# An FFT filter followed by a gated feed-forward network: another order of the loads, the filter loaded step by step, the last transform stage of the first batch two iterations later

## The chip, the cores and the metric

The kernel runs on one core of one Trainium2 chip. The metric is the device time of one execution in microseconds (us); the median of several executions is compared. A core has five engines that run side by side, each with its own queue of instructions in a fixed order: TensorE (PE in the profile; PEld are its weight loads), VectorE (DVE), ScalarE (ACT), GpSimd (POOL) and SyncE (SP), which here only issues loads and the stores of the result. Matmuls write to PSUM, and ACT or DVE bring the results from there to SBUF. Data come from and go to HBM by DMA.

## What is computed

The input `x` has 8 batches of 3136 rows of 256 numbers. Each batch is transformed along its rows, multiplied by a complex filter, transformed back, and goes through a feed-forward network with a convolution over three rows and a gate:

```python
X = np.fft.rfft(x, axis=1)
F = (filt_r + 1j * filt_i)[None, :, :]
y = np.fft.irfft(X * F, n=x.shape[1], axis=1)
...
h = np.maximum(y @ w_in, 0.0)
conv_out = np.zeros_like(h)
for k in range(K):
    conv_out += conv_w[k][None, None, :] * hp[:, k:k + S, :]
gate = 1.0 / (1.0 + np.exp(-conv_out))
return (h * gate @ w_out).astype(np.float32)
```

Here `hp` is `h` with a row of zeros at each end. The weights `w_in`, `conv_w` and `w_out` arrive as 64-bit floats; the kernel turns them into 32-bit floats itself.

## The kernel before

The kernel has two parts. The forward part does the transforms and the filter for all eight batches; the feed-forward part then goes through the result in 28 blocks. This study is about the forward part and the seam between the two.

**The pipeline of the forward part.** A transform of 3136 points is done in stages, as matmuls with tables. The work is cut into pairs of columns: `NP = 14` pairs for each of 8 batches make 112 steps, and one loop with the counter `i` runs all stages at once, each on another step. With `m = i - SKEW` and `SKEW = 15`, iteration `i` does:

- `filt` of step `m - 2`: three products on DVE (L350 to L352) of the transformed rows with the filter tiles `t1_sb` and `t2_sb`, then a sum `z` on POOL (L354);
- `third` of step `m - 4` on PE (L361), with the table `i1_sb`; its result goes to `store`, an ACT copy (L305) and a DMA to `b_dram` issued by ACT;
- `first` of step `i - 1` on PE (L315), of a pair of x rows with the table `s1_sb`; `keep` brings it to the tile `turn` by ACT (L319);
- `second` of step `m - 1` on PE (L338, and L341 for a batch's last step);
- `turn` of step `m` on PE (L326), a transposition with `eye_sb`; `turned_rows` brings it to the tile `a` by ACT (L331).

A batch is transposed only when all 14 of its steps have gone through `first`, which is why `m` lags by 15. The compute engines' order is written out by hand (`manual_schedule`): it is the order of the calls in an iteration. On PE that is `third`, `first`, `second`, `turn`; on ACT `store`, `keep`, `turned_rows`, and then whatever the iteration adds. SP's loads follow the order of the program too. A load waits until its buffer is free and until an earlier load has released its semaphore.

**The loads.** A pair of x rows is `[112, 2, 256]`, and there are `XBUFS = 7` buffers. Seven pairs are loaded ahead of the loop; iteration `i` then loads pair `i + 6`, into the buffer that `first` of pair `i - 1` sets free. The table `s1_sb` comes in seven parts of four columns: four of them ahead of the loop, the others in iterations 1 to 3 (L389). Four small constants come in iteration 4 (L393 to L396). The filter comes in seven chunks of four columns, in every second iteration from 8 on: `fr` into `t1_sb[0:64]`, `fi` into `t2_sb[0:64]` (L252), and the same columns of `i1_sb` (L400). `copy_filter` makes a second copy of each part in partitions 64 to 119 by ACT (L256, and L257 with the sign changed). It is called in every second iteration from 12 on, after `turned_rows`:

```python
def copy_filter(c):
    sl = slice(4 * c, 4 * c + 4)
    nc.scalar.activation(t1_sb[64:120, sl], t1_sb[0:56, sl], AF.Copy)
    nc.scalar.activation(t2_sb[64:120, sl], t2_sb[0:56, sl], AF.Copy, scale=-1.0)
    if c == 6:
        nc.sync.dma_start(out=t1_sb[92:93, G - 1], in_=nyq)
```

Step `p` of each batch uses columns `2p` and `2p + 1` of the filter, in iteration `p + 17` for the first batch; the columns then stay for the other batches.

**The weights.** `convert_conv` and `convert_weights` are generators: each call of `next` does one small step of a conversion on DVE, ACT or POOL and returns, so that one step falls into each iteration. The convolution weights are loaded and converted in iterations 3 to 15; the other weights come in 8 blocks of two 256 KB loads, the first two of them in iteration 16, and are converted from iteration 22 on, eleven calls for a block. Two buffers `raw` serve all these loads.

**The seam.** The feed-forward part reads the finished rows `y`. For the seven later batches the last transform stage runs within the feed-forward part. For batch 0 it runs at the end of the forward loop: from iteration `done = NP * B + 2 = 114` on, `last_load` reads a piece back from `b_dram`, `last_stage` (L216 on PE) transforms it one iteration later, and `last_out` brings it to `y` one more iteration later, the upper part by ACT (L147) and the rest by DVE (L150). There are 14 pieces. The forward steps end in iteration 130 with the last `third`. The first matmuls of the feed-forward part (L178 to L180) read all of `y` of batch 0. At iteration `done` the buffers of the forward part's loads and of the conversions are given up, and `y` takes their room.

Of the kernel before, what the change touches and what calls it, by code (L numbers as in the profile page):

```python
# [13 lines left out]
AF = mybir.ActivationFunctionType  # L14
ALU = mybir.AluOpType

S = 3136
N1 = 112
N2 = 28
G = 28  # L20
D = 256
# [103 lines left out]
def tile_fft_filter_gated_ffn(  # L125
# [2 lines left out]
    x: bass.AP,  # L128
    fr: bass.AP,
    fi: bass.AP,  # L130
    nyq: bass.AP,
    w_in: bass.AP,
    conv_w: bass.AP,
    w_out: bass.AP,
# [8 lines left out]
    nc = tc.nc  # L143
# [85 lines left out]
    with (  # L229
# [13 lines left out]
            nc.gpsimd.memset(v[32:64], 0.0)  # L243
        t1_sb = fc.tile([120, G, D], F32, name="t1_sb")
        t2_sb = fc.tile([120, G, D], F32, name="t2_sb")

        rows = {}

        def load_filter(c):
            sl = slice(4 * c, 4 * c + 4)  # L250
            for t, src in ((t1_sb, fr), (t2_sb, fi)):
                nc.sync.dma_start(out=t[0:64, sl], in_=src[:, sl])  # L252

        def copy_filter(c):
            sl = slice(4 * c, 4 * c + 4)
            nc.scalar.activation(t1_sb[64:120, sl], t1_sb[0:56, sl], AF.Copy)  # L256
            nc.scalar.activation(t2_sb[64:120, sl], t2_sb[0:56, sl], AF.Copy, scale=-1.0)  # L257
            if c == 6:
                nc.sync.dma_start(out=t1_sb[92:93, G - 1], in_=nyq)

        raws = {}

# [5 lines left out]
        def convert_conv():  # L268
            n = 3 * NF
            raw = cv.tile([128, 2, 512], I32, name="raw")  # L270
            nc.sync.dma_start(out=raw[:, 0, 0:2 * n], in_=conv_w)
            yield
            em = cv.tile([128, 2, 512], I32, name="em", bufs=1)
            yield from to_f32(cw.rearrange("p k f -> p (k f)"), raw[:, 0, 0:2 * n], em[:, 0, 0:n], em[:, 1, 0:n])

        def convert_weights():

            for k in range(8):
                raw = raws.pop(k)
                em = cv.tile([128, 2, 512], I32, name="em", bufs=1)  # L280
                ws = cv.tile([128, 2, 256], F32, name="ws")
                yield from to_f32(ws.rearrange("p t n -> p (t n)"), raw.rearrange("p t n -> p (t n)"), em[:, 0], em[:, 1])
                yield
                parts = [[t.rearrange("p a b -> p (a b)")[:, 256 * k:256 * k + 256] for t in w] for w in (wi, wo)]
                for part, (wh, wl) in enumerate(parts):
                    hi_act(wh, ws[:, part])
                yield
                for part, (wh, wl) in enumerate(parts):
                    lo_pool(wl, ws[:, part], wh)
                    yield  # L290
                if k < 6:
                    load_weights(k + 2)

# [4 lines left out]
        def load(b, p):  # L298
            r = xp.tile([112, 2, D], F32, name="x", bufs=XBUFS)
            nc.sync.dma_start(out=r, in_=x[b].rearrange("(p n) d -> p n d", n=N2)[:, 2 * p:2 * p + 2])  # L300
            rows["x", b, p] = r
# [62 lines left out]
        def at(i):  # L364
            return divmod(i, NP) if 0 <= i < NP * B else None

        XBUFS = 7
        SKEW = NP + 1
        nc.sync.dma_start(out=s1_sb[:, 0:4], in_=s1[:, 0:4])
        load(0, 0)  # L370
        load(0, 1)
        for c in range(1, 4):
            nc.sync.dma_start(out=s1_sb[:, 4 * c:4 * c + 4], in_=s1[:, 4 * c:4 * c + 4])
            for p in range(2 * c, min(2 * c + 2, XBUFS)):
                load(0, p)
        csteps, wsteps = convert_conv(), convert_weights()
        done = NP * B + 2
        NI = done + N2 // 2 + 3
        with tc.manual_schedule(engines=COMPUTE):
            for i in range(NI):  # L380
                m = i - SKEW
                if i == done:
# [2 lines left out]
                    forward_pools.close()  # L385
                    yps.append(ctx.enter_context(tc.tile_pool(name="y_even", bufs=1, side="right", reuse_waits="tile")))
                    lp = ctx.enter_context(tc.tile_pool(name="lp", bufs=2, side="right", reuse_waits="tile"))
                if 1 <= i < 4:
                    nc.sync.dma_start(out=s1_sb[:, 4 * i + 12:4 * i + 16], in_=s1[:, 4 * i + 12:4 * i + 16])  # L389
                if (bp := at(i + XBUFS - 1)) and i:  # L390
                    load(*bp)
                if i == 4:
                    nc.sync.dma_start(out=eye_sb, in_=eye)  # L393
                    nc.sync.dma_start(out=s2_sb, in_=s2[:, 0:120])
                    nc.sync.dma_start(out=s2s_sb, in_=s2s[:, 0:120])
                    nc.sync.dma_start(out=m2_sb, in_=m2)  # L396
                if 8 <= i < 22 and i % 2 == 0:
                    sl = slice((i - 8) // 2 * 4, (i - 8) // 2 * 4 + 4)
                    load_filter(i // 2 - 4)
                    nc.sync.dma_start(out=i1_sb[:, sl], in_=i1[:, sl])  # L400
                if bp := at(m - 2):
                    filt(*bp)
                pt = third(*bp) if (bp := at(m - 4)) else None
# [7 lines left out]
                    keep(*at(i - 1), pf)  # L411
                if pa is not None:
                    turned_rows(*at(m), pa)
                if 3 <= i < 16:
                    next(csteps, None)
                if i == 16:
                    load_weights(0)
                    load_weights(1)
                if i >= 22:
                    next(wsteps, None)  # L420
                if 12 <= i < 26 and i % 2 == 0:
                    copy_filter(i // 2 - 6)
                c = 2 * (i - done)
                if 0 <= c - 4 < N2:
                    last_out(0, c - 4)
# [155 lines left out]
```

## Time and profile before

| | us |
|---|---|
| median of 3 runs | 1576.35 |
| lowest and highest of them | 1575.82, 1579.54 |
| the profiled execution | 1574.98 |
| its span, first to last instruction | 1573.2 |

The profile describes the profiled execution; times in it count from the start of its span. The chain of work that ended last is 94% PE and 2% DMA. The loads that matter below, with their sizes and the median time from issue to landing, are these (a KB is 1024 bytes):

| load | count | KB each | us to landing |
|---|---|---|---|
| pair of x rows | 112 | 224 | 2.9 |
| `fr`, a chunk | 7 | 256 | 8.0 |
| `fi`, a chunk | 7 | 256 | 8.2 |
| `i1`, a chunk | 7 | 210 | 7.0 |
| `s1`, a part | 7 | 196 | 6.5 |
| weights, each load | 16 | 256 | 3.5 and 3.8 |
| store to `b_dram` | 112 | 224 | 2.5 |

In a view of the waits, a row names the waiting engine, the tile and line, what it waited for, and then the total in us, the number of waits and the longest. In a view of the timeline a row has its start, its duration, the engine, the line, the operation with its tiles and shapes, and in brackets how long the engine was idle before it and what ended that. Consecutive instructions of one kind stand in one row, with their count. A matmul row's duration reaches into the next row's, because matmuls are pipelined.

### The profile page before, as it was taken

How to read it: one execution, taken by the hardware profiler on the slowest of the kernel's cores; microseconds unless marked ns; L12 is line 12 of the kernel's file. 1: busy time of each engine (PE TensorE's matmuls, PEld its weight loads, DVE VectorE, ACT ScalarE, POOL GpSimd, SP SyncE). 2: the span in 40 equal slices, each digit the busy share in tenths (PEclk: the TensorE clock that was granted, in tenths of full speed). 3: DMA queues.
4: the chain of work that ended last, by engine and by line, in shares of the span. 5: the costliest groups of instructions: out<-in, count | busy, mean ns of one | idle time of the engine just before them, and what ended most of it. 6: DMA issues, size and time to landing. Idle time of an engine off the chain costs nothing.

```text
span 1573.2 us, 27760 instructions
## 1 busy us (share of the span) xinstructions
PE 1545.7 (98%) x10320; PEld 1425.4 (91%) x10320; DVE 1280.8 (81%) x1965; ACT 1249.4 (79%) x2274; POOL 697.9 (44%) x624
## 2 busy tenths in 40 slices
PE   6999999999999999999999999999999999999998
PEld 6777887777999999999999999999999999999998
DVE  0677788778888888888888888888888888888887
ACT  4655555556988888888888888888888888888887
POOL 0455555543444444444444444444444444444444
PEclk8999999999999999999999999999999999999999
DMA  9855555544111011111101111111111111100001
GB/s 226 231 177 164 165 166 165 153 124 129 30 47 48 30 48 48 47 48 47 44 29 36 48 48 52 43 48 48 36 42 48 48 40 38 48 24 24 24 24 48
DMA packets 87209, 115.58 MB, mean 73 GB/s; under 512 B 7114, under 2 KB 59043, under 8 KB 87075
## 3 DMA queue, kind: packets, MB, share of 16 engines
q1 hardware_dynamic: 72739, 88.11, 18.8%
q10 hardware_dynamic: 14336, 25.70, 5.8%
q8 instruction: 82, 1.34, 0.4%
q14 instruction: 52, 0.43, 0.1%
HBM read 62.40 MB, written 51.38 MB: 72 GB/s over the span
## 4 chain that ended last, share of the span: by engine, by line
PE 94%; DMA 2%; ACT 1%; DVE 1%; SPq 0%; issue 0%; POOL 0%; ACTq 0%; POOLq 0%
PE ps_h L179 12%; PE ps_h L180 12%; PE ps_h L178 11%; PE po L488 11%; PE po L490 11%; PE po L489 11%; PE ps L361 6%; PE pp L338 6%; PE ps_h L216 6%; PE ps L315 5%; PE ps L326 3%; DMA t_sb<-in_fi 1%; PE ps L216 1%; DVE y L150 1%; ACT y L147 0%; DMA x<-in_x 0%
## 5 line engine op out<-in xcount | busy, mean ns | idle before, releaser
L153 POOL TENSOR_TENSOR g<-t,g 128x448 fp32r<-128x448 f32 x448 | 517.3, 1155 | 664.5 <-ACT g L147 261.4
L488 PE MATMUL po<-wo,g 128*128 128x256 f32 x1568 | 442.1, 282 | 0.0
L490 PE MATMUL po<-wo,g 128*128 128x256 f32 x1568 | 434.4, 277 | 0.0
L489 PE MATMUL po<-wo,g 128*128 128x256 f32 x1568 | 434.2, 277 | 0.0
L462 DVE SCALAR_TENSOR_TENSOR t<-ps_h,cw,t 128x448 f32<-128x448 f32 x448 | 305.7, 682 | 82.7 <-ACT t L457 72.1
L179 PE MATMUL ps_h<-y,wi 128*128 128x450 f32 x896 | 330.2, 369 | 3.9 <-DVE y L150 3.9
L178 PE MATMUL ps_h<-y,wi 128*128 128x450 f32 x896 | 329.0, 367 | 2.0 <-DVE t L468 1.8
L180 PE MATMUL ps_h<-y,wi 128*128 128x450 f32 x896 | 328.6, 367 | 0.0
L463 DVE SCALAR_TENSOR_TENSOR t<-ps_h,cw,t 128x448 f32<-128x448 f32 x448 | 306.5, 684 | 16.0
L457 ACT ACTIVATE t<-ps_h,cw 128x448 f32<-128x448 f32 x448 | 284.8, 636 | 42.1 <-ACT ps_h L455 1.1
L488 PEld LDWEIGHTS po<-wo,g 128*128 128x128 f32 x1568 | 294.9, 188 | 6.9
L489 PEld LDWEIGHTS po<-wo,g 128*128 128x128 f32 x1568 | 294.6, 188 | 5.6
L490 PEld LDWEIGHTS po<-wo,g 128*128 128x128 f32 x1568 | 294.7, 188 | 0.0
L468 DVE TENSOR_TENSOR t<-ps_h,t 128x448 f32<-128x448 f32 x448 | 275.3, 614 | 0.1
L455 ACT ACTIVATE ps_h<-ps_h 128x450 f32<-128x450 f32 x448 | 251.6, 562 | 29.3 <-PE ps_h L180 24.6
L467 ACT ACTIVATE t<-t 128x448 f32<-128x448 f32 x448 | 255.0, 569 | 12.2 <-DVE t L463 11.0
L147 ACT ACTIVATE g<-t 128x448 fp32r<-128x448 f32 x448 | 254.6, 568 | 0.2 <-DVE t L468 0.2
L354 POOL TENSOR_TENSOR z<-u,v 120x512 f32<-120x512 f32 x112 | 157.2, 1404 | 186.4 <-DVE v L352 171.9
L180 PEld LDWEIGHTS ps_h<-y,wi 128*128 128x128 f32 x896 | 168.2, 188 | 13.7
L179 PEld LDWEIGHTS ps_h<-y,wi 128*128 128x128 f32 x896 | 168.2, 188 | 12.5 <-DVE y L150 5.9
L178 PEld LDWEIGHTS ps_h<-y,wi 128*128 128x128 f32 x896 | 170.2, 190 | 10.2 <-DVE t L468 2.9
L150 DVE TENSOR_TENSOR y<-ps_h,y 128x448 fp32r<-128x448 f32 x98 | 103.3, 1054 | 77.1 <-ACT y L147 77.1
(54 smaller groups left out, 1661.5 us busy)
## 6 DMA issues: line engine op xcount, KB each, us to landing
x<-in_x SPq DMA_DIRECT2D x112, 224.0 KB, 2.9
b_dram<-sb ACTq DMA_DIRECT2D x112, 224.0 KB, 2.5
br<-b_dram SPq DMA_DIRECT2D x112, 224.0 KB, 2.6
out<-ot SPq DMA_DIRECT2D x27, 896.0 KB, 4.1
raw<-in_w_in SPq DMA_DIRECT2D x8, 256.0 KB, 3.5
raw<-in_w_out SPq DMA_DIRECT2D x8, 256.0 KB, 3.8
t_sb<-in_fr SPq DMA_DIRECT2D x7, 256.0 KB, 8.0
t_sb<-in_fi SPq DMA_DIRECT2D x7, 256.0 KB, 8.2
```

What stands on the lines that cost most here:

```text
L153: nc.gpsimd.tensor_tensor(out=dst, in0=src, in1=hi.bitcast(F32), op=ALU.subtract)
L178: nc.tensor.matmul(ps, lhsT=wh, rhs=rh, start=start, stop=False, **kw)
L179: nc.tensor.matmul(ps, lhsT=wh, rhs=rl, start=False, stop=False, **kw)
L180: nc.tensor.matmul(ps, lhsT=wl, rhs=rh, start=False, stop=stop, **kw)
L457: nc.scalar.activation(t, h[:, 1:SUB + 1], AF.Copy, scale=cw[:, 1, f:f + 1])
L462: nc.vector.scalar_tensor_tensor(out=t, in0=h[:, 0:SUB], scalar=cw[:, 0, f:f + 1], in1=t, op0=ALU.mult, op1=ALU.add)
L463: nc.vector.scalar_tensor_tensor(out=t, in0=h[:, 2:SUB + 2], scalar=cw[:, 2, f:f + 1], in1=t, op0=ALU.mult, op1=ALU.add)
L467: nc.scalar.activation(t, t, AF.Sigmoid)
L468: nc.vector.tensor_mul(t, h[:, 1:SUB + 1], t)
L488: nc.tensor.matmul(o, lhsT=gh[:, sl], rhs=wo[0][:, f], start=first, stop=False, skip_group_check=True)
L489: nc.tensor.matmul(o, lhsT=gh[:, sl], rhs=wo[1][:, f], start=False, stop=False, skip_group_check=True)
L490: nc.tensor.matmul(o, lhsT=gl[:, sl], rhs=wo[0][:, f], start=False, stop=last, skip_group_check=True)
```

## The change

The order of the loads, their sizes and some places in the loop change. No stage computes anything else, except at one point named below.

- **First loads.** `s1` and the x rows are issued in turn by one function, two pairs of x rows after each part of `s1`, from the first to the last part.
- **Constants.** `eye` and `s2` are loaded in iteration 8 instead of 4, `s2s` and `m2` in iteration 16.
- **Filter.** It is loaded by steps of two columns instead of chunks of four, one step in each iteration from 10 to 23. `fi` goes into partitions 0 to 55 of `t2_sb`, as before but without the eight rows of padding. `fr` goes into partitions 64 to 119 of `t1_sb`; only for the last step is it loaded into both halves, as the two differ there (so the separate load of `nyq` goes). The copy of `fi` to the other half stays on ACT; the copy of `fr`, now from the upper to the lower half, moves to DVE. Both are made in iteration `p + 16`, one before the step is used. The rows 32 to 63 of `t1_sb` are set to zero by POOL at the start.
- **Weights.** The convolution weights are loaded in iteration 26, with two iterations of pause, and get eight calls. Five of these now do a conversion step; the last three of the eight steps (two on DVE, one on POOL), which add the lowest bits, are not reached. The other weights are loaded from iteration 30 and converted from iteration 35, ten calls for a block instead of eleven: the two subtractions on POOL fall into one iteration.
- **Last stage of batch 0.** `done` is 116 instead of 114. The loop has two iterations more.

```diff
+        nc.gpsimd.memset(t1_sb[32:64], 0.0)
...
-        def load_filter(c):
-            sl = slice(4 * c, 4 * c + 4)
-            for t, src in ((t1_sb, fr), (t2_sb, fi)):
-                nc.sync.dma_start(out=t[0:64, sl], in_=src[:, sl])
+        def load_filter(p):
+
+            sl = slice(2 * p, 2 * p + 2)
+            nc.sync.dma_start(out=t2_sb[0:56, sl], in_=fi[0:56, sl])
+            nc.sync.dma_start(out=t1_sb[64:120, sl], in_=fr[64:120, sl])
+            if p == NP - 1:
+                nc.sync.dma_start(out=t1_sb[0:56, sl], in_=fr[0:56, sl])
+            nc.sync.dma_start(out=i1_sb[:, sl], in_=i1[:, sl])
...
+        def copy_filter(p):
+            sl = slice(2 * p, 2 * p + 2)
             nc.scalar.activation(t2_sb[64:120, sl], t2_sb[0:56, sl], AF.Copy, scale=-1.0)
-            if c == 6:
-                nc.sync.dma_start(out=t1_sb[92:93, G - 1], in_=nyq)
+            if p < NP - 1:
+                nc.vector.tensor_copy(t1_sb[0:56, sl], t1_sb[64:120, sl])
...
-            yield
+            for _ in range(3):
+                yield
...
                 for part, (wh, wl) in enumerate(parts):
                     lo_pool(wl, ws[:, part], wh)
-                    yield
+                yield
...
+        def load_first(i):
+            if i < NP and i % 2 == 0:
+                nc.sync.dma_start(out=s1_sb[:, 2 * i:2 * i + 4], in_=s1[:, 2 * i:2 * i + 4])
+            if bp := at(i):
+                load(*bp)
+
+        for i in range(XBUFS):
+            load_first(i)
         csteps, wsteps = convert_conv(), convert_weights()
-        done = NP * B + 2
+        done = NP * B + 4
...
-                if (bp := at(i + XBUFS - 1)) and i:
-                    load(*bp)
-                if i == 4:
+                if i:
+                    load_first(i + XBUFS - 1)
+                if i == 8:
                     nc.sync.dma_start(out=eye_sb, in_=eye)
                     nc.sync.dma_start(out=s2_sb, in_=s2[:, 0:120])
+                if 10 <= i < 10 + NP:
+                    load_filter(i - 10)
+                if i == 16:
                     nc.sync.dma_start(out=s2s_sb, in_=s2s[:, 0:120])
                     nc.sync.dma_start(out=m2_sb, in_=m2)
-                if 8 <= i < 22 and i % 2 == 0:
-                    sl = slice((i - 8) // 2 * 4, (i - 8) // 2 * 4 + 4)
-                    load_filter(i // 2 - 4)
-                    nc.sync.dma_start(out=i1_sb[:, sl], in_=i1[:, sl])
...
-                if 3 <= i < 16:
+                if 0 <= m - 1 < NP:
+                    copy_filter(m - 1)
+                if 26 <= i < 34:
                     next(csteps, None)
-                if i == 16:
+                if i == 30:
                     load_weights(0)
                     load_weights(1)
-                if i >= 22:
+                if i >= 35:
                     next(wsteps, None)
-                if 12 <= i < 26 and i % 2 == 0:
-                    copy_filter(i // 2 - 6)
```

More of the change, by code (lines that the diff above doesn't have):

```diff
@@ L245, in tile_fft_filter_gated_ffn @@
         t2_sb = fc.tile([120, G, D], F32, name="t2_sb")
+        nc.gpsimd.memset(t1_sb[32:64], 0.0)
         rows = {}
-        def load_filter(c):
-            sl = slice(4 * c, 4 * c + 4)
-            for t, src in ((t1_sb, fr), (t2_sb, fi)):
-                nc.sync.dma_start(out=t[0:64, sl], in_=src[:, sl])
-        def copy_filter(c):
-            sl = slice(4 * c, 4 * c + 4)
-            nc.scalar.activation(t1_sb[64:120, sl], t1_sb[0:56, sl], AF.Copy)
+        def load_filter(p):
[7 more added lines that the diff above has]
+            sl = slice(2 * p, 2 * p + 2)
             nc.scalar.activation(t2_sb[64:120, sl], t2_sb[0:56, sl], AF.Copy, scale=-1.0)
-            if c == 6:
-                nc.sync.dma_start(out=t1_sb[92:93, G - 1], in_=nyq)
+            if p < NP - 1:
+                nc.vector.tensor_copy(t1_sb[0:56, sl], t1_sb[64:120, sl])
         raws = {}
@@ L368, in tile_fft_filter_gated_ffn @@
         SKEW = NP + 1
[L369 to L375, printed above, removed]
+        def load_first(i):
[5 more added lines that the diff above has]
+            load_first(i)
         csteps, wsteps = convert_conv(), convert_weights()
-        done = NP * B + 2
+        done = NP * B + 4
         NI = done + N2 // 2 + 3
@@ L387, in tile_fft_filter_gated_ffn @@
                     lp = ctx.enter_context(tc.tile_pool(name="lp", bufs=2, side="right", reuse_waits="tile"))
-                if 1 <= i < 4:
-                    nc.sync.dma_start(out=s1_sb[:, 4 * i + 12:4 * i + 16], in_=s1[:, 4 * i + 12:4 * i + 16])
-                if (bp := at(i + XBUFS - 1)) and i:
-                    load(*bp)
-                if i == 4:
+                if i:
+                    load_first(i + XBUFS - 1)
+                if i == 8:
                     nc.sync.dma_start(out=eye_sb, in_=eye)
                     nc.sync.dma_start(out=s2_sb, in_=s2[:, 0:120])
+                if 10 <= i < 10 + NP:
+                    load_filter(i - 10)
+                if i == 16:
                     nc.sync.dma_start(out=s2s_sb, in_=s2s[:, 0:120])
                     nc.sync.dma_start(out=m2_sb, in_=m2)
-                if 8 <= i < 22 and i % 2 == 0:
-                    sl = slice((i - 8) // 2 * 4, (i - 8) // 2 * 4 + 4)
-                    load_filter(i // 2 - 4)
-                    nc.sync.dma_start(out=i1_sb[:, sl], in_=i1[:, sl])
                 if bp := at(m - 2):
@@ L550 @@
     bins = _bins()
-    fr, fi = np.zeros((2, 64, G, D), np.float32)
-    fr[:56] = filt_r[bins]
-    fi[:56] = filt_i[bins]
+    fr = np.zeros((120, G, D), np.float32)
+    fr[:56] = fr[64:] = filt_r[bins]
+    fr[92, G - 1] = filt_r[S // 2]
+    fi = filt_i[bins]
     fi[28, G - 1] = 0.0
@@ L558 @@
         "fi": fi,
-        "nyq": filt_r[S // 2:S // 2 + 1],
         "w_in": moe_w_in.reshape(KT, 128, FF).transpose(1, 0, 2).reshape(128, -1),
```

1 line of the change is left out of this document (removed).

## The prediction

> **What bounds the kernel now.** I read the busy times, then the 20 us windows, then who waited for whom, then the timeline of the stretches that stand out.
>
> ```profile
> PE 1545.7 (98%) x10320; PEld 1425.4 (91%) x10320; DVE 1280.8 (81%) x1965; ACT 1249.4 (79%) x2274; POOL 697.9 (44%) x624
> ...
> 0.00:20.00 20.00, 14.45 (x85) 14.09 (x86) 1.16 (x7) 6.92 (x12) 1.51 (x8) 0.97 0.93 232
> 20.00:40.00 20.00, 13.54 (x65) 11.63 (x64) 2.07 (x3) 9.97 (x14) 0.89 (x1) 0.69 1.05 220
> 40.00:60.00 20.00, 19.94 (x118) 15.58 (x117) 14.69 (x23) 14.18 (x23) 8.31 (x7) 1.00 0.96 248
> 60.00:80.00 20.00, 17.50 (x96) 13.30 (x94) 13.60 (x21) 13.55 (x22) 7.89 (x5) 0.91 0.78 219
> ```
>
> A window's columns are length, busy time of PE, PEld, DVE, ACT, POOL, granted clock, DMA share, GB/s. TensorE (PE) is busy 98% of the span; 14.6 us of its 27.5 idle us lie in the first 80 us (5.55+6.46+0.06+2.50), where the DMA share is near 1. The loads are the limit of that stretch. How they reach PE:
>
> ```profile
> PE pp L338 <- ACT a L331: 7.6, 2, 5.1
> ...
> ACT t_sb L256 <- DMA t_sb<-in_fr: 5.2, 3, 2.0
> ACT t_sb L257 <- DMA t_sb<-in_fi: 2.5, 3, 1.5
> ```
>
> PE's largest wait is for ACT's evacuation of the turned rows (7.6 us, two waits). ACT itself stood 7.7 us before the filter copies of `copy_filter`, which lie ahead of that evacuation in its queue.
>
> ```profile
> 16.06 1.11 PE L315 MATMUL ps<-s_sb,x 112*128 112x112 f32 x8 [0.53 <-DMA x<-in_x]
> 17.87 8.89 PE L315 MATMUL ps<-s_sb,x 112*128 112x112 f32 x48 [0.69 <-ACT turn L319]
> 28.11 0.70 PE L326 MATMUL ps<-eye_sb,turn 128*112 128x128 f32 x4 [1.35 <-ACT turn L319]
> ...
> 42.88 1.03 PE L361 MATMUL ps<-z,i_sb 120*112 120x256 f32 x4
> ...
> 84.47 1.03 PE L361 MATMUL ps<-z,i_sb 120*112 120x256 f32 x4
> 85.34 1.04 PE L315 MATMUL ps<-s_sb,x 112*128 112x112 f32 x8
> ...
> 87.52 1.03 PE L361 MATMUL ps<-z,i_sb 120*112 120x256 f32 x4
> ```
>
> The eight matmuls at 16.06 are `first` of row pair 8, those to 26.8 pairs 9 to 14; 28.11 is the first `turn` (i=15), 42.88 the first `third` (i=19), 87.52 the fourteenth (i=32). One iteration without a wait takes 87.52 - 84.47 = 3.05 us, of which a `third` is 85.34 - 84.47 = 0.87. Thirteen of them are 39.7 us; the kernel takes 87.52 - 42.88 = 44.6. So I predict when the first and the fourteenth `third` start. The fourteenth needs the last filter step, and after it nothing in the head is late.
>
> **The change, part by part.**
>
> *Order of the first loads.* Four constants and the convolution weights leave the stretch before row pair 11, and row pairs take turns with `s1`. By the tiles' sizes `s1` comes in parts of 196 KB, a row pair is 224 KB. Three rates, over x and s1 alone, over filters and x, over filters, x and stores:
>
> ```profile
> 8.00:14.00 6.00, 6.00 (x38) 6.00 (x38) 0.00 (x0) 2.52 (x5) 0.00 (x0) 1.00 1.07 264
> 28.00:48.00 20.00, 14.72 (x77) 11.35 (x78) 8.27 (x12) 12.19 (x19) 3.81 (x3) 0.83 1.04 211
> 54.00:60.00 6.00, 6.00 (x36) 4.55 (x35) 4.66 (x9) 2.92 (x6) 2.84 (x2) 1.00 1.01 284
> ```
>
> Pair 8 landed at 16.06, with six parts of `s1` and nine pairs ahead of it or with it: 3192 KB. In the new order pair 14 is there after seven parts and fifteen pairs, 4732 KB; the 1540 KB between (1.58 MB) take 6.0 us at 264 GB/s: 22.0 us. `first(14)` follows, then `turn`. Three iterations without `third` (3 x 2.18) and the first turn bring the first `third` to about 30 us if PE runs at full clock. The before run had clock 0.69 in 20 to 40, and its six groups from 17.87 took 8.89 us, 1.48 each against 0.87 at full clock. Waiting for each pair again leaves gaps, so I allow half of the worst, 2 us or so: 32.5 us instead of 42.88.
>
> *Filter by steps, one step per iteration from i=10.* A step is x 224, fi 112, fr 112, i1 105 KB: 553 KB or 0.566 MB. It removes a 256 KB load per part and chunk (64 rows, 8 of them padding), and adds queue slots: 43 loads for 21, all on SP, each before the x row of the next iteration. Step 0 lands after eye, s2 and pairs 15 and 16: 893 KB after pair 14, 4.3 us at 211 GB/s, so at 26.3; step 2 two steps later, 2 x 2.68, at 31.7. From then on stores take 224 KB per 3.05 us, 75 GB/s. At 284 GB/s in all a step takes 0.566/(284-75) = 2.71 us, at 211 it takes 4.16; the ends are far apart. I take the row of 40 to 60, in which filters, weights and stores run as they will here, 248: 3.27 us. The last of eleven further steps lands at 61.5, 67.7 or 77.5.
>
> The Trainium skill speaks to this at two places, and they disagree. "SBUF — State Buffer", section "Door 1: The DMA port swizzle", says that partitions 0 to 63 reach half of the sixteen DMA ports and 64 to 127 the other half. The 211 GB/s of a stretch with both filter parts in partitions 0 to 63 agrees with a limit there; by that rule `fr` into 64 to 119 relieves it. "DMA: Bandwidth & Descriptors", section "Rules for kernel authors", says that two transfers to disjoint halves serialize, because each already spreads over all sixteen engines; by it nothing is gained. No row of before has both halves loading, so it stays open.
>
> *Copies.* ACT loses fourteen copies of 1.05 us with their waits and gains fourteen of half the size; DVE gains thirteen of 56x512, POOL a memset of 32x7168.
>
> ```profile
> L354 POOL TENSOR_TENSOR z<-u,v 120x512 f32<-120x512 f32 x16 | 22.2, 1386 | 47.0 <-DVE v L352 47.0
> ...
> L351 DVE TENSOR_TENSOR v<-pp,t_sb 56x512 f32<-56x512 f32 x16 | 10.9, 683 | 0.4
> ...
> L305 ACT ACTIVATE sb<-ps 112x512 f32<-112x512 f32 x14 | 8.4, 597 | 1.4 <-PE ps L361 1.3
> L256 ACT ACTIVATE t_sb<-t_sb 56x1024 f32<-56x1024 f32 x7 | 7.4, 1056 | 5.3 <-DMA t_sb<-in_fr 5.2
> L257 ACT ACTIVATE t_sb<-t_sb 56x1024 f32<-56x1024 f32 x7 | 7.3, 1046 | 2.5 <-DMA t_sb<-in_fi 2.5
> ...
> L243 POOL MEMSET v<- 32x512 f32 x2 | 1.0, 516 | 0.1
> ```
>
> A DVE copy has no row; between nothing and the 0.68 of a two-input product of the same shape I take 0.68. Three products and a copy are then 2.75 us of 3.05, so PE's period hides it; without that cover it costs 13 x 0.68 = 9 us. ACT's copy is half of 1.05, beside store, keep and evacuation of about 0.6 each: 2.3 of 3.05. The memset is 14 x 0.516 = 7.2 us on an idle POOL, over by about 10 us, needed by the first product near 27. Both copies wait for their step of the filter, and queued behind them on ACT are the next store and evacuation, on DVE the next `filt`; PE waits for those. From a step's landing to its `third` go ACT 0.6, three products 2.07, POOL 1.4 and some gaps: 4.4 us. So the fourteenth `third` is at 67.7 + 4.4 = 72.1 by the loads (65.9 and 81.9 at the ends), and at 32.5 + 39.7 = 72.2 by PE. Two limits so close hinder each other; I add 1 us: 73.2, and the gain of the head is 87.5 - 73.2 = 14.3 us.
>
> *Weights later.* Loads at i=30, conversions from i=35, ten calls a block instead of eleven, ending at i=115. PE's period hides the same DVE work, one call in each iteration as before; cover gone, it would be up to 0.7 us in each of some 60 iterations. The second weight load waits for a slot that the convolution weights hold until i=32, with x rows queued behind it on SP; those are loaded six iterations ahead, so at most three iterations of hold cost nothing. The convolution weights lose their last three small instructions, beside the path.
>
> *Last stage two iterations later.* The tail of the forward part:
>
> ```profile
> 383.14 1.28 POOL L354 TENSOR_TENSOR z<-u,v 120x512 f32<-120x512 f32 x1 [1.75 <-DVE v L352]
> ...
> 383.58 0.98 ACT L147 ACTIVATE y<-ps 128x448 fp32r<-128x448 f32 x1 [0.39 <-ACT sb L305]
> ...
> 384.48 2.05 PE L361 MATMUL ps<-z,i_sb 120*112 120x256 f32 x4 [1.92 <-POOL z L354]
> 384.59 0.98 DVE L150 TENSOR_TENSOR y<-ps,y 128x448 fp32r<-128x448 f32 x1 [0.61 <-ACT y L147]
> ...
> 385.96 0.94 PE L178 MATMUL ps_h<-y,wi 128*128 128x450 f32 x1
> ```
>
> Now the last z ends at 384.42, the last `third` waits for it, and the last y is done at 385.57 beside it; the feed-forward part begins at 385.96. After the change two iterations before the last z lose a last stage (0.87 each, the cost of a `third`'s slot), so z is ready 1.7 us earlier, near 382.7. But behind the last `third` (1.03 us, 2.05 when the clock has dropped) then come ACT's store 0.60, two y rounds of 0.98 and DVE's 0.98, with 0.5 us between them: 382.7 + 1.03 + 0.60 + 1.96 + 0.98 + 0.5 = 387.8, or 388.8 cold. That is 1.8 to 2.8 us later, and PE, idle for some 3 us, starts the next part on a lower clock, bound between 0 and the 1 us that the cold `third` lost. I take 2.8 us; if DVE is late by its backlog as now, up to 4.
>
> **Sum**: -14.3 + 2.8 = -11.5 us. The profiled execution took 1574.98 us around its span of 1573.2, 1.4 under the median 1576.35 of the three runs; from that median, 1565 us.
>
> **Rivals.**
>
> A, my forecast: loads and PE meet as above. 1565 (1562 to 1569). For it: the rates of three stretches. Chance 0.56.
>
> B, the opposite halves relieve the loads, or PE keeps its clock: PE alone sets the pace, `third` from 31, the fourteenth at 71, gain 16.5, tail 2.8: 1562.5. For it, 211 GB/s with filters against 264 without. Chance 0.28.
>
> C, the split does not do what it says: 211 GB/s holds with stores too, the last step lands at 77.5, `third` at 81.9: gain 5.6, less 2.8: 1573.5, no change. Against it, 284 GB/s with stores beside filters. Chance 0.12.
>
> D, slower: small rows (i1's halve to 896 bytes, fi's and fr's to 2 KB) make the loads crawl. Then ACT and DVE stop at every step's copy. It decides where the fourteenth `third` passes 84.7 (the gain under 2.8): step 4.4 us, 0.795 MB with its store in that time, 180 GB/s. At 160 GB/s a step takes 5 us, `third` is at 91: 3.5 + 2.8 = 6 us slower, 1582.5. No 20 us window of the head is under 219. Chance 0.04.
>
> **How the numbers follow.** 1565 is A's. The range takes in B with a row order that works better still (1560.5) and reaches from A half way towards C (1570.5). About 0.3%, 4.7 us, is what a measurement of this kernel can tell from no change: A and B are faster, C is within it, D slower: faster 0.84, same 0.12, slower 0.04.
>
> **What would show it.** Right: no PE wait for ACT near 30 and 61; the first `third` at 31 to 34, the fourteenth at 71 to 75; the clock above 0.69 in 20 to 40; near 370 a `third`, one last stage, then some 3 us without PE. Wrong: the filter copies waiting for DMA in most steps (C, D), DVE's copies at 1 us or more, PE idle in 80 to 330, a tail under 1 us. If x rows came no sooner than before, the first term would fall by 4 us.

## The result, and the profile after

| | before | after |
|---|---|---|
| median, in runs side by side | 1576.41 | 1567.12 |
| lowest and highest | 1575.82, 1579.54 | 1562.93, 1568.01 |
| the profiled execution | 1574.98 | 1568.01 |
| its span | 1573.2 | 1566.2 |

The ratio after to before is 0.9932 [0.991, 0.9954]: 9.3 us less by the medians, where 11.5 less was forecast. Between the two profiled executions it is 7.0 us, and the readings below explain these 7.0. The four runs of after lie 5 us apart, and the profiled one is the slowest of them. Two executions far slower than the others of their kernel (3125.22 us of before, 1918.42 of the kernel with late copies) are left out of the comparisons below. PE is busy for 98% of the span, as before. The windows of 20 us of after, with the same columns as before:

```profile
0.00:20.00 20.00, 14.68 (x98) 14.03 (x99) 0.00 (x0) 8.02 (x14) 7.29 (x8) 1.00 0.94 246
20.00:40.00 20.00, 19.78 (x127) 15.99 (x127) 13.58 (x22) 13.69 (x24) 5.69 (x5) 1.00 0.90 224
40.00:60.00 20.00, 19.48 (x115) 14.93 (x114) 15.41 (x23) 14.77 (x26) 7.51 (x7) 1.00 0.83 234
60.00:80.00 20.00, 16.19 (x82) 12.30 (x82) 12.39 (x21) 9.53 (x17) 7.42 (x6) 0.87 0.78 246
```

The stretch from 20 to 40 us is mended: PE is busy 19.78 us instead of 13.54, at a granted clock of 1.00 instead of 0.69. From 60 to 80 PE is busy less than before (16.19 against 17.50) and the clock falls to 0.87. So something new stands in the way there. The view of PE's waits over the whole span, after:

```profile
PE ps L319 <- DMA x<-in_x: 6.2, 5, 4.1
PE ps L365 <- POOL z L358: 5.4, 5, 2.9
...
PE ps_h L177 <- ACT y L146: 2.0, 1, 2.0
```

The same view of before has, for x rows and `z`:

```profile
PE ps L315 <- DMA x<-in_x: 4.9, 2, 4.3
...
PE ps L361 <- POOL z L354: 3.0, 2, 1.9
```

The wait for ACT's evacuation of the turned rows (7.6 us before) is gone. The wait for `z` has grown from 3.0 to 5.4 us, with one of 2.9, and one of 2.0 for `y` is new. The timeline of PE shows where the first belongs (L365 is `third`, the line that was L361):

```profile
29.80 1.03 PE L365 MATMUL ps<-z,i_sb 120*112 120x256 f32 x4
...
65.25 1.12 PE L365 MATMUL ps<-z,i_sb 120*112 120x256 f32 x4 [0.23 <-POOL z L358]
68.45 1.03 PE L365 MATMUL ps<-z,i_sb 120*112 120x256 f32 x4
75.48 2.05 PE L365 MATMUL ps<-z,i_sb 120*112 120x256 f32 x4 [2.87 <-POOL z L358]
...
81.57 1.08 PE L365 MATMUL ps<-z,i_sb 120*112 120x256 f32 x4
...
84.67 1.03 PE L365 MATMUL ps<-z,i_sb 120*112 120x256 f32 x4
```

The first `third` is at 29.80, 13.08 us earlier than before. The thirteenth is at 68.45, so the fourteenth would be at 71.50, a period of 3.05 us later. It comes at 75.48, after an idle of 2.87 us, and then runs at a lower clock (0.50 from 75.5 to 81.5 us): its four matmuls take 2.05 us instead of 1.03, and the iteration to the fifteenth takes 6.09 us instead of 3.05. The sixteenth is at 84.67. Before, with the fourteenth at 87.52 and two periods of 3.05, it is due at 93.62: the head has gained 8.95 us. What `z` waited for stands in the timelines of DVE and of SP, after (an SP row is the issue of a load):

```profile
71.65 0.18 DVE L160 TENSOR_SCALAR em<-raw 128x24 int32<-128x24 int32 x1 [5.32 <-DMA raw<-in_conv_w]
71.86 0.69 DVE L354 TENSOR_TENSOR u<-pp,t_sb 120x512 f32<-120x512 f32 x1
```

```profile
67.51 0.35 SPq L274 DMA_DIRECT2D raw<-in_conv_w  x1
```

The first conversion step of the convolution weights (L160, a step of 0.18 us) stood in DVE's queue for 5.32 us, ahead of the products of the last filter step. The program places the load in iteration 26, but SP issued it at 67.51, between the twelfth and the thirteenth `third`: PE was in iteration 30. The step that needs it is placed in iteration 29, so the three iterations from 26 to 29 had been used up before the load was on its way. Why SP ran so late was not tested; what it waited for most in the first 85 us, ahead of its x loads, was PE (9.7 us), then stores (7.3) and earlier x loads (6.8).

The tail of the forward part, from the timeline of PE after, and the row of before that answers to its last line:

```profile
373.88 1.12 PE L365 MATMUL ps<-z,i_sb 120*112 120x256 f32 x4 [1.05 <-POOL z L358]
...
377.86 0.47 PE L177 MATMUL ps_h<-y,wi 128*128 128x450 f32 x1 [1.98 <-ACT y L146]
378.93 0.74 PE L178 MATMUL ps_h<-y,wi 128*128 128x450 f32 x1 [0.61 <-DVE y L149]
```

```profile
386.69 0.58 PE L179 MATMUL ps_h<-y,wi 128*128 128x450 f32 x1
```

The last `third` (373.88) is no longer late by a backlog of DVE, but behind it PE waits twice for `y`. The second matmul of the feed-forward part starts 7.76 us earlier than before, so the tail has given back 8.95 - 7.76 = 1.2 us. The spans differ by 7.0: another 0.8 is lost behind it. There PE's clock is still low where in before it had risen again, as a window of after and the window of before at about the same place behind the second matmul show:

```profile
380.00:384.00 4.00, 4.00 (x17) 3.61 (x16) 1.37 (x2) 2.25 (x5) 0.00 (x0) 0.75 0.00 0
```

```profile
388.00:392.00 4.00, 3.92 (x20) 3.26 (x18) 2.44 (x4) 3.36 (x7) 0.00 (x0) 1.00 0.19 57
```

The granted clock is 0.75 here and was 1.00, which fits the 0.8 us; that it makes up all of it is not shown.

### The profile page after: what moved, and what is told of

Same layout as the page of the kernel before. It is cut to its first block, busy times and chain, and to the rows that moved or that the text cites. A ratio compares the mean times of both kernels' runs of the same rounds, so it can differ in the third digit from the quotient of the medians.

```text
span 1566.2 us, 27791 instructions
## 1 busy us (share of the span) xinstructions
PE 1541.9 (98%) x10320; PEld 1419.9 (91%) x10320; DVE 1288.1 (82%) x1976; ACT 1246.0 (80%) x2274; POOL 704.9 (45%) x624
## 4 chain that ended last, share of the span: by engine, by line
PE 95%; DMA 2%; DVE 2%; ACT 1%; POOL 0%; issue 0%; SPq 0%; ACTq 0%; POOLq 0%; DVEq 0%
PE ps_h L178 12%; PE ps_h L179 12%; PE ps_h L177 11%; PE po L491 11%; PE po L493 11%; PE po L492 11%; PE ps L365 6%; PE pp L342 6%; PE ps_h L215 6%; PE ps L319 5%; PE ps L330 3%; DMA x<-in_x 1%; DVE y L149 1%; PE ps L215 1%; ACT y L146 1%; PE pp L345 0%
## 5 line engine op out<-in xcount | busy, mean ns | idle before, releaser
L465 DVE SCALAR_TENSOR_TENSOR t<-ps_h,cw,t 128x448 f32<-128x448 f32 x448 | 305.6, 682 | 83.9 <-ACT t L460 73.2
```

Of the source, the lines that this page charges most:

```text
L465: nc.vector.scalar_tensor_tensor(out=t, in0=h[:, 0:SUB], scalar=cw[:, 0, f:f + 1], in1=t, op0=ALU.mult, op1=ALU.add)
```

## The experiments

Twelve runs follow, one of them the changed kernel again. My theory after the result: the head gained what was forecast, and 6 us of it fell to DVE's wait for the convolution weights (2.87 idle and 3.04 of low clock). The rival: at the fourteenth `third` the filter or the x rows would have been late anyway. A second question is which part of the change brought the gain.

**The convolution weights loaded ten iterations earlier** (from after):

```diff
-                if 26 <= i < 34:
+                if i == 16 or 27 <= i < 34:
```

> The changed kernel with one load moved: the convolution weights are loaded in iteration 16 instead of 26, their conversion steps stay in iterations 29 to 33 (the lowest bits are left out as in the changed kernel). Theory: in the changed kernel DVE stood 5.3 us before this load (issued at 67.5 us, because SP ran late), with the filter products of the last filter step queued behind it; PE lost 2.9 us of waiting and 3.0 us of low clock in the next iteration. Then DVE's wait goes, the fourteenth third starts near 72 us instead of 75.5, the next ones follow at 3.05 us, and the time falls by 5 to 6 us, from 1567 to about 1561.5. Rival: the x rows and filter steps are late by themselves at that place; then another DMA wait takes its place and the time falls by less than 2 us.

Measured: 1561.04 (1560.15 to 1561.36), ratio to before 0.9911 [0.9898, 0.9924]. That is some 6 us under after, and 5.7 under its repetition below, whose interval lies clear of this one (that of the first measurement of after does not). The timelines of this kernel, PE's and DVE's, then SP's:

```profile
29.96 1.03 PE L365 MATMUL ps<-z,i_sb 120*112 120x256 f32 x4
...
71.84 1.03 PE L365 MATMUL ps<-z,i_sb 120*112 120x256 f32 x4
...
74.89 1.03 PE L365 MATMUL ps<-z,i_sb 120*112 120x256 f32 x4
...
367.16 1.12 PE L365 MATMUL ps<-z,i_sb 120*112 120x256 f32 x4 [1.04 <-POOL z L358]
...
372.21 0.47 PE L178 MATMUL ps_h<-y,wi 128*128 128x450 f32 x1 [0.59 <-DVE y L149]
```

```profile
66.44 0.18 DVE L160 TENSOR_SCALAR em<-raw 128x24 int32<-128x24 int32 x1
```

```profile
41.67 0.42 SPq L274 DMA_DIRECT2D raw<-in_conv_w  x1
```

The same conversion step, at the same place in DVE's queue, has no wait before it (no bracket). The fourteenth `third` is at 71.84 and the fifteenth 3.05 us later. The rival, that another wait for a load takes its place, falls. SP issued this load, placed in iteration 16, at 41.67: 11.7 us, or four periods, after the first `third` (29.96), which belongs to iteration 19. So it was about seven iterations late, and only the distance of thirteen iterations to its use made it harmless.

**The kernel after, run again**, beside the other experiments:

> The changed kernel once more, on the chip of these runs, to have its spread. If DVE's wait before the convolution weights is what costs, its time varies with that wait: runs between 1562 and 1568 with a profile that shows the wait; a run without it would lie near 1561.

Measured: 1566.78 (1564.05 to 1568.99), ratio 0.995 [0.9938, 0.9962]. Its profile has the same wait:

```profile
74.06 2.04 PE L365 MATMUL ps<-z,i_sb 120*112 120x256 f32 x4 [3.67 <-POOL z L358]
...
78.86 1.03 PE L365 MATMUL ps<-z,i_sb 120*112 120x256 f32 x4
```

The fastest of the five, 1564.05, is the profiled one, and it has the wait, even a longer one; so the wait alone does not make the spread. Here the iteration behind it takes 4.80 us instead of 6.09, and behind the seam the granted clock is 1.00 from 372 to 384 us, where after has 0.83 from 376 to 380 and 0.75 from 380 to 384. How long the clock stays low differs from execution to execution, which may account for some of the 5 us between runs.

**`fr` into the same half as `fi`**, as before the change, on top of the earlier convolution weights; DVE copies upward:

```diff
-            nc.sync.dma_start(out=t1_sb[64:120, sl], in_=fr[64:120, sl])
+            nc.sync.dma_start(out=t1_sb[0:56, sl], in_=fr[0:56, sl])
...
-                nc.vector.tensor_copy(t1_sb[0:56, sl], t1_sb[64:120, sl])
+                nc.vector.tensor_copy(t1_sb[64:120, sl], t1_sb[0:56, sl])
```

> As the run with the early convolution weights, but both filter parts are loaded into partitions 0 to 55 and DVE copies fr upward instead of downward; sizes, order and number of the loads are the same. Theory that opposite halves relieve the loads: filter steps land later, the GB/s in 24 to 44 us fall below 215, the fourteenth third starts 2 to 6 us later than in that run, and the time is 2 to 6 us longer. Rival, that the halves do not matter: both within 1 us.

Measured: 1563.31 (1561.26 to 1566.7), ratio 0.9927 [0.9914, 0.994]. Windows 24 to 44 and 40 to 60 with opposite halves (the kernel above), and then with the same half:

```profile
24.00:44.00 20.00, 20.00 (x121) 15.67 (x119) 17.24 (x26) 14.96 (x27) 7.08 (x6) 1.00 0.82 216
40.00:60.00 20.00, 19.50 (x113) 14.85 (x112) 16.66 (x25) 14.88 (x27) 7.40 (x7) 1.00 0.86 247
```

```profile
24.00:44.00 20.00, 19.23 (x115) 14.76 (x113) 16.51 (x24) 13.96 (x25) 7.14 (x6) 1.00 0.89 210
40.00:60.00 20.00, 19.13 (x107) 13.70 (x105) 16.95 (x23) 13.84 (x25) 7.74 (x6) 1.00 0.88 240
```

The opposite halves bring 3% in bytes per second (216 for 210, 247 for 240), and 2.3 us in the medians; the intervals of the two ratios overlap, so the time is an indication. In the traces the same half has its fourteenth `third` at 73.18 instead of 71.84: 1.3 us later, where 2 to 6 were expected. The DMA share tells more than the bytes: it is 0.89 and 0.88 with the same half, 0.82 and 0.86 with opposite halves, so that per busy time 12% and 5% more bytes move (216/0.82 against 210/0.89, 247/0.86 against 240/0.88). PE was busy for 19.13 us or more of each window, so little of this reached it. The Trainium skill, "SBUF — State Buffer", section "Can I just issue two DMAs to hit both halves?", says that two transfers to opposite halves serialize and gave only 6% more than one: the gain here, in mixed traffic, is small too. No stretch of these runs shows a doubling.

**One part alone: the copies of the filter four iterations later in the queue** (from before; the loads stay as they were):

```diff
-                if 12 <= i < 26 and i % 2 == 0:
-                    copy_filter(i // 2 - 6)
+                if 16 <= i < 30 and i % 2 == 0:
+                    copy_filter(i // 2 - 8)
```

> The kernel before with one edit: the filter copies on ACT are made in iterations 16 to 28 instead of 12 to 24, just before they are used; all loads, their order and sizes are as before. Theory that the place of the copies in ACT's queue cost most: PE's 7.6 us of waits for ACT's evacuation shrink below 2, the first third starts near 35 to 37 us instead of 42.9, and the time falls by 6 to 11 us. Rival, that the order and the amount of the loads were the cost: the filter chunks stay late, PE waits for them in another row, and the time falls by less than 4 us.

Measured: 1568.95 (1566.3 to 1572.62), ratio 0.9964 [0.9951, 0.9976], 5.7 us less than before, between what the theory and its rival expected. The first `third` is at 35.34, as expected. PE's largest wait is now another:

```profile
PE ps L315 <- DMA x<-in_x: 13.2, 9, 4.4
```

The wait for ACT's evacuation is gone, and in its place PE waits for x rows: 13.2 us in nine waits, where before has 4.9 in two waits. Moving one call brings more than half as much as the whole change (5.7 us against 9.3 by the medians, or 10.7 by the ratio), and what PE waits for then are x rows, which SP issues in turn with the filter.

**One part alone: the order of the first loads** (from before; `load_first` and the places of the constants as in the change). **And both of these parts together.**

> The kernel before with the order of the first loads alone changed: x rows and s1 in turn, eye and s2 in iteration 8, s2s and m2 in iteration 16; the convolution weights stay in iteration 3, the filter in chunks with its copies where they were. Theory that a queue in fixed order behind a late load is what costs, and that ACT's copies hold it back wherever the x rows are: the waits of PE for ACT stay above 4 us and the time falls by 0 to 3 us. Rival, that the order of the first loads was the main cost, as my first term had it: the first third comes 5 us or more before 42.9 and the time falls by 5 us or more.

> The kernel before with two parts: the new order of the first loads, and the copies late as in the earlier run with late copies; filter still in chunks in the lower half, weights still loaded in iteration 16. Theory: the two parts add up only now, since ACT no longer stands behind the filter; the first third comes near 31 us, and the time falls by 8 to 11 us; what is left to the run with early convolution weights (13.8 us) is due to steps, halves and later weights. Rival: the late copies alone were all, and the time falls by 5 to 6 us as with them alone.

Measured: the order alone 1575.22 (1574.03 to 1578.28), ratio 1.0007 [0.9999, 1.0016]; both 1570.68 (1566.18 to 1572.57), ratio 0.9976 [0.9963, 0.9988]. Waits of ACT up to 90 us in the first kernel, the first `turn` in its timeline, and a wait in the second:

```profile
ACT t_sb L256 <- DMA t_sb<-in_fr: 9.7, 3, 4.3
```

```profile
28.37 1.11 PE L326 MATMUL ps<-eye_sb,turn 128*112 128x128 f32 x4 [5.15 <-ACT turn L319]
```

```profile
29.17 2.02 PE L315 MATMUL ps<-s_sb,x 112*128 112x112 f32 x8 [4.01 <-DMA x<-in_x]
```

The earlier x rows alone bring nothing: PE comes to the first `turn` earlier and waits 5.15 us there, because ACT's wait for `fr` has grown from 5.2 to 9.7 us. Both parts together bring 3.8 us, not more than the copies alone; the waits for x rows stay (11.6 us in six waits), and the first `third` is at 39.04, not near 31. I had expected the two gains to add, and they don't. What I took from this, and the next runs try, is that the stretch has a limit that neither part touches: the bytes ahead of the x rows in SP's queue.

**The other weights loaded during the filter** (from the first experiment; the convolution weights have a buffer of their own here, so that they don't hold one of `raw`):

```diff
-                if i == 30:
+                if i == 17:
                     load_weights(0)
                     load_weights(1)
```

> The run with early convolution weights, but the first two blocks of weights (1 MB) are loaded in iteration 17 instead of 30, while the filter is still loading; the convolution weights have a tile of their own so that no slot is awaited; conversions as there. Theory that every byte that is not needed yet holds back the filter and x rows while the queues are full: the fourteenth third comes 2.5 to 4 us later and the time grows by 2 to 5 us. Rival, that PE is the limit there and has slack: the time stays within 1 us.

**The filter in chunks of four columns again, every second iteration, from iteration 10; and the same from iteration 8:**

```diff
-            sl = slice(2 * p, 2 * p + 2)
+            sl = slice(2 * p, 2 * p + 4)
...
-                if 10 <= i < 10 + NP:
+                if 10 <= i < 10 + NP and i % 2 == 0:
```

> The run with early convolution weights, but the filter loaded in chunks of four columns in every second iteration (rows of 4 KB, half as many loads); halves, copies and all else as there. Theory that steps matter, since a chunk of 658 KB ahead of an x row holds that row back: PE's waits for x rows grow from 0.8 us to 3 us or more beyond the first 4.1, and the time by 2 to 6 us. Rival, that larger loads move faster: the time falls by up to 2 us, or stays within 1 us.

> The run with chunks, but the filter loads start in iteration 8 instead of 10, as in the kernel before; nothing else differs. With the order of the first loads and the late copies alone, PE waited 4.0 us at 29 us for an x row and the first third came at 39.0; with chunks from iteration 10 it came at 32.2. Theory that the early start of the filter holds back the x rows before they are ahead: the wait for an x row near 29 us is 3 us or more, the first third comes 3 to 7 us later than 32.2, and the time is 2 to 5 us longer than 1560.8. Rival, that the weights loaded in iteration 16 were the whole rest: first third and time as in the run with chunks, within 1 us.

Measured: weights in iteration 17, 1565.48 (1564.77 to 1570.01), ratio 0.9948 [0.9935, 0.9961]; chunks from 10, 1560.81 (1559.96 to 1562.89), ratio 0.9913 [0.9899, 0.9926]; chunks from 8, 1564.19 (1563.67 to 1566.53), ratio 0.9935 [0.9922, 0.9949]. In the kernel with the early weights, SP's timeline and PE's:

```profile
44.10 0.36 SPq L304 DMA_DIRECT2D x<-in_x  x1
...
49.14 0.43 SPq L269 DMA_DIRECT2D raw<-in_w_out  x1
49.67 0.37 SPq L304 DMA_DIRECT2D x<-in_x  x1
```

```profile
56.50 2.02 PE L319 MATMUL ps<-s_sb,x 112*128 112x112 f32 x8 [5.49 <-DMA x<-in_x]
```

Between two x rows the filter step and four weight loads (1 MB) pass SP, 5.6 us, and PE later waits 5.49 us for an x row: weights beside the filter cost 4.4 us against the first experiment by the medians. (The profiled execution was the slowest of its five; its fourteenth `third` comes at 79.82, 8 us later.) The size of a load does not show in the time, 1560.81 with chunks and 1561.04 with steps, so my theory that steps matter missed; in the traces the chunks bring the first `third` 2.2 us later (32.20) and the fourteenth 1.0 later (72.83). Starting the filter two iterations earlier costs 3.4 us by the medians; in that kernel's timeline an x row is late already in the first stretch:

```profile
26.19 1.67 PE L320 MATMUL ps<-s_sb,x 112*128 112x112 f32 x8 [3.38 <-DMA x<-in_x]
```

There the first `third` is at 34.60, 2.4 us later than with chunks from 10 and a little less than expected, and the fourteenth at 74.27, 1.4 later. So the direction is shown, and the 3.4 us are an indication.

From "order and copies" to the first experiment, 9.6 us of medians, the runs show these parts: weights out of the filter's stretch 4.4, filter from iteration 10 instead of 8 3.4, opposite halves 2.3, steps instead of chunks nothing, less the later last stage (below), 1.7. That sums to 8.4; the rest is within the spread of the medians. These are the prices of one edit each, beside the others in place, and as prices of parts need not add, the sum is a rough one.

**The last stage alone two iterations later** (from before):

```diff
-        done = NP * B + 2
+        done = NP * B + 4
```

> The kernel before with one edit: the last stage of batch 0 starts in iteration 116 instead of 114; nothing else moves. My step: the time grows by 1.8 to 2.8 us (1578.2 to 1579.2), with PE waiting about 2 us for the last y rounds before the feed-forward part. Rival: DVE works without a gap at the tail and sets its end either way; then the time stays within 0.5 us.

Measured: 1576.2 (1574.28 to 1579.37), ratio 1.0011 [1.0002, 1.0019], or +1.7 us by the ratio. PE's waits have the row that the change brought too:

```profile
PE ps_h L178 <- ACT y L147: 2.0, 1, 2.0
```

From the fourteenth `third` to the second matmul of the feed-forward part it takes 300.4 us here (84.72 to 385.11) and 299.2 in before (87.52 to 386.69): 1.2 more. The two profiled executions end their spans at 1573.3 and 1573.2 nevertheless, because the fourteenth `third` of this one came 2.8 us sooner, with nothing changed up to there. So single executions of one head differ by that much.

**Two versions to beat both.** With `done` at 114 the buffers are given up two iterations earlier, so all conversions have to end earlier. The first version loads the convolution weights in iteration 16 and begins to use them in iteration 20, a distance of four; the second loads them in iteration 12, into a buffer of their own, and uses them from iteration 25, a distance of thirteen. In both they are converted in full, all eight steps, and the other weights are loaded in iteration 27 and converted from 33 on.

```diff
-        done = NP * B + 4
+        done = NP * B + 2
...
-                if 26 <= i < 34:
+                if i == 16 or 18 <= i < 28:
```

> The changed kernel with three edits: convolution weights loaded in iteration 16 and converted in full in iterations 20 to 27, weights loaded from iteration 27 and converted from 33, so that the last stage of batch 0 can start in iteration 114 as in the kernel before. Theory: on top of the 6 us of the early convolution weights the tail gives back its 1.9 us, about 1559 beside 1561 of that run. Rival: an earlier conversion puts new waits on DVE in iterations 20 to 35, and the time is that of that run or more.

```diff
-            raw = cv.tile([128, 2, 512], I32, name="raw")
+            raw = cv.tile([128, 2 * n], I32, name="craw", bufs=1)
...
-                if 26 <= i < 34:
+                if i == 12 or 23 <= i < 33:
```

> The changed kernel with the convolution weights in a tile of their own, loaded in iteration 12 and converted in full from iteration 25, weights loaded from iteration 27 and converted from 33, last stage of batch 0 from iteration 114. The earlier try at this loaded the convolution weights in iteration 16 and needed them in 20; SP issued that load at 43.5 us and DVE stood 7.9 us. Theory, that the distance in time from issue to use decides, not the place in the program: here about 20 us lie between, DVE does not wait, and the time is 1.9 us under the run with early convolution weights, near 1559. Rival: the earlier start of the last stage or the earlier weights bring a wait of their own, and the time is 1561 or more.

Measured: the first 1567.77 (1567.34 to 1570.94), ratio 0.996 [0.9948, 0.9973]; the second 1559.85 (1558.38 to 1560.21), ratio 0.9903 [0.9888, 0.9918]. The first missed, as its rival said, and the timeline of DVE and of PE says why:

```profile
45.42 0.18 DVE L160 TENSOR_SCALAR em<-raw 128x24 int32<-128x24 int32 x1 [7.87 <-DMA raw<-in_conv_w]
```

```profile
49.23 2.05 PE L365 MATMUL ps<-z,i_sb 120*112 120x256 f32 x4 [6.30 <-POOL z L358]
```

I had walked into the same wait, 26 us earlier in the span: the load of iteration 16 is issued when PE is some seven iterations further, and four iterations of distance don't cover that. The second has no such wait, and its tail is that of before:

```profile
72.02 1.03 PE L365 MATMUL ps<-z,i_sb 120*112 120x256 f32 x4
...
75.08 1.03 PE L365 MATMUL ps<-z,i_sb 120*112 120x256 f32 x4
...
369.00 1.70 PE L365 MATMUL ps<-z,i_sb 120*112 120x256 f32 x4 [1.94 <-POOL z L358]
...
370.87 0.58 PE L178 MATMUL ps_h<-y,wi 128*128 128x450 f32 x1
```

From the fifteenth `third` to the second matmul of the feed-forward part it takes 370.87 - 75.08 = 295.8 us, and in the first experiment, with `done` at 116, 372.21 - 74.89 = 297.3: the tail alone is worth 1.5. This version is the fastest version that ran, 14.5 us under before by the medians of runs side by side, although it does three conversion steps that the change leaves out. That it also beats the first experiment (0.9911) isn't settled: the intervals overlap.

## Why the prediction came out as it did

The time forecast was 1565.0 and the measured median is 1567.1: the sign and the size hold, but partly by luck. The head did not go as forecast A has it, with loads and PE meeting; it went as in rival B, at PE's pace and faster than forecast, and then lost 7.0 us to a wait that no part of the forecast has. These errors partly cancel.

- **The first `third`**: forecast at 32.5, measured 29.80. The step "Waiting for each pair again leaves gaps, so I allow half of the worst, 2 us or so" was too careful: the granted clock from 20 to 40 us was 1.00. The gain of the first term was 13.1 us instead of 10.4.
- **From the first to the fourteenth `third`**: forecast 40.7, measured 45.7. Without the wait it would be 71.50 - 29.80 = 41.7, and the first experiment has its fourteenth at 71.84. So 73.2, forecast for a kernel without that wait, was 1.4 to 1.7 us too late: near in size, but for another reason than A gives, as PE was busy for 19.78 and 19.48 us of the windows 20 to 40 and 40 to 60.
- **The step that failed** is in *Weights later*: "The convolution weights lose their last three small instructions, beside the path", with "after it nothing in the head is late". I counted DVE's steps and had the load leave the first stretch, but left out where it arrives: in SP's queue in iteration 26, behind the filter, with its first step in DVE's queue ahead of the last products. I had looked at SP's queue for the other weights only. It cost 3.98 us up to the fourteenth `third` (75.48 - 71.50) and 3.04 behind it.
- **The filter loads**: I took 248 GB/s between 211 and 284. Measured 224 from 20 to 40 and 234 from 40 to 60, at a DMA share of 0.90 and 0.83: with PE busy as above, the loads were not the limit there.
- **Copies**: with 0.68 for a DVE copy I was on the safe side (median 0.42, but three of thirteen took 1.00 to 1.48, below); the memset took 6.07 us (7.2 forecast). DVE's load hid in PE's period as forecast.
- **The tail**: forecast +2.8 us at the start of the feed-forward part, bound to 1.8 to 2.8 plus up to 1 for the clock. Measured +1.2 there and +2.0 by the end of the span; alone +1.7, interval 0.3 to 3. The mechanism was right: `third` earlier (367.16 in the first experiment against 369.00 in the fastest version), then two waits for `y`. The price was over-sized by 0.8.
- **The rivals**: B, PE alone, had the fourteenth `third` at 71. That is about where the first experiment stands, and with the wait taken away the time is 13.8 us under before in runs side by side (1561.04 against 1574.8), which is B's gain of 13.7 (16.5 - 2.8). For the reason that B names first, the opposite halves, the runs show only some 1 to 2 us. C and D asked for filter copies that wait for DMA in most steps: on ACT 4 of 14 waited, 2.1 us in all, on DVE 6 of 13, 4.3 us without the first, and PE was never idle from 80 to 330.

In one line, between the two profiled executions: -13.1 for the first `third`, +1.0 up to the fourteenth, +3.0 for the iteration behind it, +1.2 for the tail, +0.8 behind that; sum -7.1, measured -7.0. The forecast for the same terms was -10.4, -3.9, 0 and, for the last two together, +2.8: it was 2.7 us too careful on the first, and short by 5.0 and by 3.0 on the next two.

## What to carry to other kernels

For a load that is moved, ask on which engine its first user stands, what is queued behind that user, and how late the issuing queue runs in that stretch: "loaded three iterations ahead" counted in the program was issued four iterations late on the chip, while thirteen iterations ahead cost nothing. An instruction of 0.18 us ahead of the critical product costs as much as the wait that it brings. And parts of a change don't add: the earlier x rows brought nothing, the later copies 5.7 us, both together no more (3.8), until the filter and the weights had left their way.

## What the runs showed of the hardware that was not expected

**A short idle of PE brings a second loss.** Behind 2.87 us of idle the four matmuls of `third` took 2.05 us instead of 1.03, and the iteration 6.09 instead of 3.05; behind 3.67 us in the repetition of after 4.80, and behind 6.30 us in the first of the two versions above 4.83 (49.23 to 54.06). So the second loss does not grow with the idle. It does not always come either: the 1.98 us of idle at the seam are followed by a granted clock of 0.83 and 0.75 in after, and of 1.00 in the repetition.

**A DVE copy and GpSimd's sum wait for each other.** DVE's copies of `fr` by their line, then three of them in the timeline of DVE after, and POOL's rows beside the last two:

```profile
L262 DVE COPY t_sb<-t_sb x13: 415/422/1477, 25.1 to 63.6; 56x512 f32<-56x512 f32 x13
```

```profile
25.11 0.42 DVE L262 COPY t_sb<-t_sb 56x512 f32<-56x512 f32 x1 [25.11 <-DMA t_sb<-in_fr]
...
28.03 1.45 DVE L262 COPY t_sb<-t_sb 56x512 f32<-56x512 f32 x1 [0.26 <-DMA t_sb<-in_fr]
...
31.63 0.42 DVE L262 COPY t_sb<-t_sb 56x512 f32<-56x512 f32 x1
```

```profile
27.92 1.27 POOL L358 TENSOR_TENSOR z<-u,v 120x512 f32<-120x512 f32 x1 [20.04 <-DVE v L356]
...
31.79 1.39 POOL L358 TENSOR_TENSOR z<-u,v 120x512 f32<-120x512 f32 x1 [2.60 <-DVE v L356]
```

The columns of the first row are the least, median and longest duration in ns. Alone a copy takes 0.42 us; begun at 28.03, with POOL's `z` running from 27.92 to 29.19, it ends at 29.48, that is 0.29 behind POOL's end. The other copies of after follow the same pattern. Two more began while a `z` ran (42.35 and 60.47) and ended 0.28 and 0.29 us behind its end. Three had no `z` beside them, and seven began just before a `z`; all of these took 0.41 or 0.42. And in those seven cases it is `z` that ends late, 1.13 or 1.14 us behind the end of the copy whenever it began: at 31.63 the copy ends at 32.05, `z` at 33.18. So the one that begins second ends a fixed time behind the end of the first. The Trainium skill, "SBUF — State Buffer", section "Who interferes with whom", says that DVE and GpSimd share a pair of ports under an exclusive lock: these copies agree with that. A two-input product on DVE, one of whose inputs (`pp`) lies in PSUM, does not show it: 0.69 us at 74.23, beside a `z` of POOL from 74.16. That one holds up the other is shown by the order of the rows; that it is by a pair of ports is the page's, not shown.
